# An adaLN block (grouped-KV attention and a ReLU feed-forward): a rewritten start and a rewritten end around an unchanged main loop

## The chip, the cores and the metric

The kernel runs on one core of a Trainium2 chip. A core has five engines that run side by side, each through its own instruction queue in order: TensorE (PE, the matmuls; the loads of its stationary operand are listed apart as PEld), VectorE (DVE), ScalarE (ACT), GpSimd (POOL) and SyncE (SP, which here only starts DMAs). Matmuls write to PSUM, eight banks of 128 x 512 floats; the other engines take the results from there. The metric is the device time of one execution in microseconds (us), the median of several runs. A profile of one execution gives busy times, waits and the TensorE clock that was granted, as a share of full speed.

## What is computed

```python
mod = (silu(c) @ w_mod).reshape(1, 6, 1, 512)       # c: (1, 512), w_mod: (512, 3072)
sa, ca, ga, sb, cb, gb = mod[:, 0] ... mod[:, 5]
h = layernorm(x) * (1 + ca) + sa                    # x: (1, 2048, 512)
# attention: 32 query heads of 16, one head of keys and values for all of them
q, k, v = h @ wq, h @ wk, h @ wv
o = softmax(q @ k.T / 4) @ v
x = x + ga * (o @ wo)
h = layernorm(x) * (1 + cb) + sb
x = x + gb * (relu(h @ w1) @ w2)                    # w1: (512, 1792), w2: (1792, 512)
```

Everything is float32. The kernel keeps that accuracy on the faster matmul type by splitting operands into a high and a low part and adding three products (high x high, high x low, low x high).

## The kernel before

**Tiling.** The 2048 rows are handled in 4 blocks of 512 for the first layer norm and the projections (names `xb1`, `hT`, `kv`, `qproj`), and in 8 blocks of 256 for everything after the attention. A unit `u` is one of 8 query blocks times 4 groups of 8 heads, 32 units in all. A unit needs 64 row maxima (one matmul of 48 x 512 and one DVE reduction over 512 each, `max_of`), then 64 score matmuls with an exponential on ACT (`scores`), and matmuls of the exponentials with the values (`values`).

**Main loop.** 256 cycles `c`, each with 8 maxima for the next unit, 8 scores with their exponentials, 8 matmuls of values, and a portion of "other" work on PE (`behind`: the output projection, second layer norm and feed-forward of the block before). The order within a cycle is written out by hand in `PARTS`: each letter pops one step (a and b a maximum, c and d a score, u and l a portion of other work, V the values, P the steps that were put off, t the transposes). All five engines run exactly in the order of the program text.

**The start (head).** Before the loop: first layer norm, keys and values, the first queries, the six modulation vectors, all 64 maxima of unit 0 and some of unit 1 (`LEAD`, 24). Its order is the string `HEAD`: k is the next step of the generator `first()` (transposes, keys and values, query projections, modulation vectors), n one of `norms()`, m a pair of maxima, w two idle matmuls. The statistics of a row block come from DVE (`ln1_sums`); the inverse root from an integer first guess on DVE and three Newton steps, on POOL (`ln_stats` with `late` false) or on DVE (`late` true). Maxima use three PSUM banks (`ps_max`); the modulation vectors and query projections use the single bank `ps_fill`.

**The end (tail).** `normalise` of the last unit fetches the softmax denominators with small DMAs, all on SP. `behind_last` then does the last block of 256 rows with nothing beside it but the second half of the block before (`second(1)`, 42 matmuls): split of the attention output (`parts`), output projection (24 matmuls), layer norm of one tile of 128 rows after the other, transposes, first layer (14 pieces `f` of 12 matmuls, `dense1`, whose weights `w1s` are fetched by `load_w1` into three buffers), second layer (84 matmuls, `dense2`), `close_block` (residual and store).

**Second modulation.** The scale (1 + cb) and shift sb lie as full tiles `cbr` and `sbr`, made by `mod_all` with a row matmul and a broadcasting matmul each, and `normed` multiplies and adds them row-wise, two operations of 128 x 512 per tile.

The functions that the change touches, and what calls them:

## Time and profile before

| | |
|---|---|
| median of 3 runs | 1687.48 us (1687.15 to 1687.67) |
| the profiled execution, its own time | 1693.38 us |
| its span (first to last record) | 1691.6 us |
| PE busy | 1656.8 us (98% of the span) |
| DVE busy | 1348.8 us (80%) |
| ACT busy | 1229.8 us (73%) |
| POOL busy | 348.0 us (21%) |
| mean granted TensorE clock | 0.982 |
| first score matmul of the loop starts at | 125.35 us |
| last matmul of values ends near | 1607 us |

The span falls into three stages: the head to 125.35 us, the loop to about 1607 us, and the tail to 1691.6 us. A stage table gives for each stretch its length, then for each engine the busy time and the number of instructions, then the granted clock, the busy share of the DMA engines and the rate. A chain row gives a start, a length and the work that the next step waited for. A wait row gives the waiting line, what released it, the total, how often and the longest.

### The profile page before, as it was taken

To read this page: it belongs to the slowest core of one execution; us is meant where nothing else is said; L and a number is where in the kernel's file an instruction comes from. 1 tells how busy PE (TensorE), PEld (TensorE's weight loads), DVE (VectorE), ACT (ScalarE), POOL (GpSimd) and SP (SyncE) were. 2 spreads that over 40 slices of the span, in tenths; PEclk is the share of its full clock that TensorE was granted. 3 is DMA by queue.
4 is the path that set the end of the run, shared out by engine and by line. 5 is a ranking of instruction groups with operands and counts; after the bars stand their busy time and mean duration, and the time that the engine had idled before them with its cause. 6 is when DMAs were issued, how large, how long until landed. Compare 5 with 4: busy or idle time off the path is not lost.

```text
span 1691.6 us, 34294 instructions
## 1 busy us (share of the span) xinstructions
PE 1656.8 (98%) x13196; PEld 967.6 (57%) x13196; DVE 1348.8 (80%) x2327; ACT 1229.8 (73%) x2414; POOL 348.0 (21%) x472
## 2 busy tenths in 40 slices
PE   8899999999999999999999999999999999999987
PEld 6445555555655566556655565556655665556566
DVE  6568888898888888898888888888888888984031
ACT  3318888878877788778877887778877887778710
POOL 3201345431101311121103111131113110221110
PEclk9779999999999999999999999999999999999999
DMA  7122644212301131113311131104211230113132
GB/s 251 54 57 81 198 153 117 89 59 73 105 29 58 34 115 55 35 41 97 91 29 36 59 104 41 59 17 121 66 35 41 85 104 19 45 47 106 30 118 98
DMA packets 86514, 129.13 MB, mean 76 GB/s; under 512 B 24964, under 2 KB 52548, under 8 KB 86352
## 3 DMA queue, kind: packets, MB, share of 16 engines
q1 hardware_dynamic: 84664, 126.85, 24.1%
q8 instruction: 106, 1.74, 0.4%
q14 instruction: 56, 0.46, 0.1%
q10 hardware_dynamic: 1688, 0.08, 0.1%
HBM read 99.94 MB, written 24.76 MB: 74 GB/s over the span
## 4 chain that ended last, share of the span: by engine, by line
PE 92%; DVE 4%; DMA 2%; ACT 1%; POOL 1%; issue 0%; SPq 0%; POOLq 0%; DVEq 0%; ACTq 0%
PE ps_pv L966 29%; PE ps_max L491 22%; PE ps_fill L195 18%; PE ps_exp L785 15%; DVE pm L493 2%; PE ps_max L178 1%; PE ps_exp L178 1%; DMA w1s<-w1dr 1%; PE ps_exp L354 1%; PE ps_fill L178 1%; DVE st L242 1%; PE ps_pv L169 1%; PE ps_exp L329 0%; PE ps_fill L214 0%; ACT pe L787 0%
## 5 line engine op out<-in xcount | busy, mean ns | idle before, releaser
L493 DVE TENSOR_REDUCE pm<-ps_max 128x1 f32<-128x512 f32 x2048 | 1273.1, 683 | 192.2 <-PE ps_fill L195 103.2
L787 ACT ACTIVATE pe<-ps_exp 128x512 f32<-128x512 f32 x2048 | 1081.6, 605 | 297.4 <-PE ps_fill L195 199.9
L491 PE MATMUL ps_max<-kp,qp 48*128 48x512 f32 x2048 | 817.6, 430 | 8.9 <-DVE pm L493 8.7
L785 PE MATMUL ps_exp<-qp,kp 50*128 50x512 f32 x2048 | 746.4, 405 | 0.6 <-ACT pe L787 0.5
L491 PEld LDWEIGHTS ps_max<-kp,qp 48*128 48x128 f32 x2048 | 374.6, 187 | 471.1 <-DVE pm L493 432.6
L966 PE MATMUL ps_pv<-pe,vt 128*32 128x512 f32 x4096 | 546.4, 605 | 0.0
L785 PEld LDWEIGHTS ps_exp<-qp,kp 50*128 50x128 f32 x2048 | 381.9, 187 | 20.8 <-ACT pe L787 5.3
L195 PE MATMUL ps_fill<-w2r,r 64*128 64x512 f32 x1044 | 290.2, 409 | 0.0
L195 PE MATMUL ps_fill<-hh,w1s 64*128 64x256 f32 x1568 | 237.8, 291 | 0.0
L195 PEld LDWEIGHTS ps_fill<-hh,w1s 64*128 64x128 f32 x1568 | 197.3, 185 | 13.4 <-issue 10.1
L195 PEld LDWEIGHTS ps_fill<-w2r,r 64*128 64x128 f32 x1044 | 178.8, 185 | 12.7 <-issue 4.2
L966 PEld LDWEIGHTS ps_pv<-pe,vt 128*32 128x32 f32 x4096 | 80.6, 108 | 126.8 <-issue 119.6
L275 POOL TENSOR_TENSOR r<-stg,r 128x512 fp32r<-128x512 f32 x49 | 63.0, 1285 | 327.8 <-ACT r L274 327.8
L195 PE MATMUL ps_fill<-hl,w1s 64*128 64x256 f32 x784 | 125.3, 280 | 0.0
L195 PE MATMUL ps_fill<-hT,wq 64*128 64x256 f32 x416 | 115.8, 407 | 0.0
L195 PEld LDWEIGHTS ps_fill<-hl,w1s 64*128 64x128 f32 x784 | 107.0, 188 | 0.0
L195 PEld LDWEIGHTS ps_fill<-hT,wq 64*128 64x128 f32 x416 | 70.4, 188 | 2.9
L1011 POOL TENSOR_TENSOR on<-num,den 128x256 f32<-128x256 f32 x31 | 22.8, 735 | 226.5 <-DMA den<-recs 175.1
L801 POOL COPY num<-pvs 128x256 f32<-128x256 f32 x32 | 12.8, 399 | 171.4 <-ACT pvs L797 171.4
L275 POOL TENSOR_TENSOR hl<-stg,hh 128x512 fp32r<-128x512 f32 x14 | 18.0, 1283 | 122.6 <-ACT hh L274 122.6
L282 ACT ACTIVATE stg<-ps_fill 128x512 f32<-128x512 f32 x62 | 38.3, 619 | 0.0
L295 POOL TENSOR_TENSOR x<-stg,x 128x512 f32<-128x512 f32 x14 | 18.1, 1292 | 96.5 <-ACT stg L294 96.5
(163 smaller groups left out, 950.7 us busy)
## 6 DMA issues: line engine op xcount, KB each, us to landing
w1s<-w1dr SPq DMA_DIRECT2D x112, 512.0 KB
qp<-qdr SPq DMA_DIRECT2D x124, 96.0 KB
qdr<-qq SPq DMA_DIRECT2D x45, 256.0 KB
raw<-in_B_w_dram SPq DMA_DIRECT2D x28, 256.0 KB
w1dr<-w1s SPq DMA_DIRECT2D x14, 512.0 KB
wmod<-in_w_mod_dram SPq DMA_DIRECT2D x6, 1024.0 KB
x<-in_A_x_dram SPq DMA_DIRECT2D x8, 512.0 KB
out_dram<-ot SPq DMA_DIRECT2D x16, 256.0 KB
```

The lines of the kernel that those rows point to most:

```text
L169: nc.tensor.matmul(pt[:, 0:P], idn, idn, start=True, stop=True)
L178: nc.tensor.matmul(pt, w, a, start=start, stop=stop)
L195: ins = nc.tensor.matmul(pt, w[r], a[r], start=start and h == 1, stop=stop and h == 0)
L275: (eng or nc.gpsimd).tensor_tensor(lo, src, hi.bitcast(F32), op=OP.subtract)
L282: nc.scalar.activation(stg, pt, func, **kw)
L295: nc.gpsimd.tensor_tensor(dst, stg, other, op=OP.add)
L491: nc.tensor.matmul(pt, qps[u][i][r, j * P:(j + 1) * P], kp[r, kb * 512:(kb + 1) * 512], start=True, stop=True)
L493: nc.vector.tensor_reduce(pms[u][:, (i * 2 + hf) * 4 + j, kb:kb + 1], pt, axis=AX.X, op=OP.max)
L785: nc.tensor.matmul(pt, kp[r, kt * P:(kt + 1) * P], qps[u][ct // 2][r], start=True, stop=True)
L787: nc.scalar.activation(pe, pt, AF.Exp)
L966: nc.tensor.matmul(pvt[i * 32:(i + 1) * 32], vt[:, kt], pes.pop((s, i)), start=(kt == 0), stop=(kt == KT - 1))
L1011: due[1]()
```

## The change

Head: a new string `HEAD` in which nearly every step is followed by a pair of maxima, with further letters: q the first queries, v the last two steps of keys and values, s and a the statistics of blocks 2 and 3, 1, 2 and 3 the normalisation of a tile of that block. The maxima rotate over four banks (`ps_pv` joins in until the loop begins), the steps over four as well (`other_bank`: three `ps_exp` and `ps_fill`). The statistics of block 3 are sums on ACT (`act_sums`: four sums, four sums of squares) instead of DVE. The inverse root is one POOL instruction with the operation pow (`power` holds -0.5) for blocks 1 to 3 and for the second layer norm in the loop; block 0 and the tail keep the Newton steps on DVE. All four normalised tiles of blocks 1 to 3 are POOL's; ACT took some before. The idle matmuls w are gone. `LEAD` is 16, and 8 further maxima of unit 1 run in the first four cycles of the loop, two in each (letter e in `PARTS`).

Second modulation: sb and 1 + cb become columns (`cols`), and `modulate` applies them after the transpose, in the loop with two POOL instructions of 128 x 256 in front of each split (`modulate_two`), in the tail on ACT and DVE.

Tail: the denominators and numerators of the last unit are fetched half by SP and half by the ACT queue, the denominators first, and the last product is on DVE. `behind_last` starts with its loads: the weights of the first 11 pieces `f` go to the three buffers `w1s` and, for 8 pieces, to buffers that held exponentials (`pe`) and queries (`qp`); the other three follow as `w1s` come free. The output projection runs the three ready head groups of both tiles first and the last group after; the layer norm handles both tiles at once; 30 of the 42 matmuls of `second(1)` stand behind the output projection and 12 behind the transposes; the second layer finishes one tile, stores it, and then does the other.

The order of instructions shows it at three places. First PE in the head, where the modulation vectors are made (`L214`/`L216` the row, `L225`/`L234` its broadcast; `L491`/`L516` a maximum; `qp_342` and `qp_451` are unit 0, `qp_739` unit 1; the number behind a bank's name is its use). Before:

```order
L225 MATMUL ps_fill_788<-mrow_780,mean_167 128x512
L491 MATMUL ps_max_791<-kp_109,qp_352 128x512
L491 MATMUL ps_max_794<-kp_109,qp_352 128x512
L214 MATMUL ps_fill_797<-wmod_97,sgb_165 32x512 x4
L491 MATMUL ps_max_804<-kp_109,qp_352 128x512
L491 MATMUL ps_max_807<-kp_109,qp_352 128x512
L225 MATMUL ps_fill_810<-mrow_802,mean_167 128x512
```

and now:

```order
L234 MATMUL ps_fill_793<-mrow_763,mean_167 128x512
L516 MATMUL ps_max_796<-kp_107,qp_451 128x512
L516 MATMUL ps_max_799<-kp_107,qp_451 128x512
L216 MATMUL ps_exp_802<-wmod_495,sgb_165 32x512 x4
L516 MATMUL ps_max_809<-kp_107,qp_451 128x512
L516 MATMUL ps_pv_812<-kp_107,qp_451 128x512
L516 MATMUL ps_max_831<-kp_107,qp_739 128x512
L516 MATMUL ps_max_834<-kp_107,qp_739 128x512
L241 MATMUL ps_exp_837<-idn_101,mrow_785 128x128 x4
```

The broadcast `ps_fill_793` now takes the row of the step before last (`mrow_763`, where `mrow_785` is the newest), other banks alternate with `ps_fill`, every second pair uses `ps_pv`, and the first maxima of unit 1 (`qp_739`) stand between the last row and the two column steps (`L241`) that took the place of two broadcasts.

Second, the DMA starts of SP at the end of the program. Before:

```order
L803 DMA num<-pvs 16x256 x4
L808 DMA den<-pvs 16x256 x4
L605 DMA out_dram<-ot 128x512
L531 DMA x_24355<-in_A_x_dram 128x2x512
L517 DMA w1s<-w1dr_113 128x1024
L517 DMA w1s<-w1dr_114 128x1024
L517 DMA w1s<-w1dr_115 128x1024
L572 DMA out_dram<-ot 128x512
L517 DMA w1s<-w1dr_116 128x1024
```

and now (the loads of `w1x` go on in the same way to `w1dr_121`):

```order
L866 DMA den<-pvs 16x256 x2
L870 DMA num<-pvs 16x256 x2
L558 DMA x_24169<-in_A_x_dram 128x2x512
L544 DMA w1s<-w1dr_111 128x1024
L544 DMA w1s<-w1dr_112 128x1024
L544 DMA w1s<-w1dr_113 128x1024
L700 DMA w1x<-w1dr_114 128x512 x2
L700 DMA w1x<-w1dr_115 128x512 x2
```

The fourth piece of weights stood behind a store that waits for the end of `second(1)`; now 8 more pieces follow the first three directly.

Third, DVE behind the last unit. Before:

```order
L1022 RECIPROCAL den<-den 128x256
L687 TENSOR_TENSOR ol<-on,oh 128x512 x2
L696 TENSOR_TENSOR x_24355<-ps_exp,x_24355 128x512
L242 BN_STATS st<-x_24355 128x6
L243 BN_AGGR mv<-st 128x2
```

and now:

```order
L868 COPY num<-pvs 128x256
L734 TENSOR_TENSOR ol<-on,oh 128x512
L734 TENSOR_TENSOR ol<-on,oh 128x256
L739 RECIPROCAL den<-den 128x256
L739 TENSOR_TENSOR on<-num,den 128x256
L734 TENSOR_TENSOR ol<-on,oh 128x256
L750 TENSOR_TENSOR x_24169<-ps_max,x_24169 128x512 x2
```

The low parts of three head groups no longer stand behind the reciprocal, the product of the last group is DVE's, and both tiles get their residual before the statistics begin.

The diff, cut to its core:

```diff
-LEAD = 24
-HEAD = ("kkmnkkmnnkkmnkmnknnnnk"
-        "kkmnkkmnnkkmkkmkkmkmk" "knnnnmkkm"
-        "kkmkmkmkmkkmkmkmkm"
-        "kmkmkmkmkmkmkmmw"
-        "kmkmkmkmmwmwmwmwmwmwmwmw")
+LEAD = 16
+HEAD = "sq11s1aa1sqmmkkkksakmvm2aq2kq2ak2mmk2kakakam3mk33km3k3mmkvmmkkkmmkkmkmkkmmvkmkmvmkmkmmkmkmkmkmkmkmkmmkmkkmmkmkkmmkkm"
-PARTS = "aucuaucPuaucuadVtbldlbldldlblbcV"
+PARTS = "aucuaucPeuaucuadVtbldlbldldelblbcV"
+NPE = 11
...
+    rot = itertools.cycle([ps_exp, ps_exp, ps_exp, ps_fill])
+    def other_bank():
+        return next(rot)()
...
+    def act_sums(b):
...
+            if t < 4:
+                nc.scalar.activation(scr, xb1[b][:, t], AF.Copy, accum_out=s1[:, t:t + 1])
+            else:
+                nc.scalar.activation(scr, xb1[b][:, t - 4], AF.Square, bias=nm[:, t - 4:t - 3],
+                                     accum_out=s2[:, t - 4:t - 3])
...
-        nc.gpsimd.tensor_scalar(nm, mv[:, :, 0], -1.0, None, op0=OP.mult)
-        for _ in range(3):
-            nc.gpsimd.tensor_tensor(u, y, y, op=OP.mult)
-            nc.gpsimd.tensor_tensor(u, u, ve, op=OP.mult)
-            nc.gpsimd.tensor_scalar(u, u, -0.5, 1.5, op0=OP.mult, op1=OP.add)
-            nc.gpsimd.tensor_tensor(y, y, u, op=OP.mult)
+        if not isinstance(mv, tuple):
+            nc.gpsimd.tensor_scalar(ve, mv[:, :, 1], EPS, None, op0=OP.add)
+            nc.gpsimd.tensor_scalar(nm, mv[:, :, 0], -1.0, None, op0=OP.mult)
+        nc.gpsimd.tensor_tensor(y, ve, power[:, 0:n], op=OP.pow)
...
-        pt = ps_max()
+        pt = next(max_banks)()
...
-            eng.tensor_tensor(xn[:, t], xn[:, t], cbr, op=OP.mult)
-            eng.tensor_tensor(xn[:, t], xn[:, t], sbr, op=OP.add)
+    def modulate(dst, src, k, eng):
+        scale, shift = cols[:, 3, k:k + 1], cols[:, 2, k:k + 1]
...
+    def modulate_two(stg, k2):
+        for k in range(2):
+            v = stg[:, k * TB:(k + 1) * TB]
+            modulate(v, v, k2 * 2 + k, nc.gpsimd)
...
+                    put_off.append(partial(modulate_two, stg, k2))
                     put_off.append(partial(split, flat(parts[0], k2), flat(parts[1], k2), stg))
...
+        ahead += [spare_w1(f, "pe", NPE, nc.sync) for f in range(3, 8)]
+        ahead += [spare_w1(f, "qp", 6, nc.sync) for f in range(8, 11)]
...
+        for t in range(TT):
+            run_all([d for n, d in enumerate(out_proj(pts[t], oo, t)) if n % DC < 3])
+        for t in range(TT):
+            run_all([d for n, d in enumerate(out_proj(pts[t], oo, t)) if n % DC == 3])
+        more(30)
...
-                if f + 3 < FC:
-                    ahead.append(load_w1(f + 3))
+                if f < 3:
+                    ahead.append(load_w1(f + 11))
...
+        if u == NU - 1:
+            nc.gpsimd.tensor_copy(den, pvs[:, TB:])
+            for c in range(4):
+                (nc.sync, nc.scalar)[c % 2].dma_start(
+                    den[c * 32:c * 32 + DH], pvs[c * 32 + DH:(c + 1) * 32, 0:TB])
+            nc.vector.tensor_copy(num, pvs[:, 0:TB])
...
-    sums = [ln1_sums(b) for b in range(NL)]
+    sums = [(ln1_sums, act_sums)[b == 3](b) for b in range(NL)]
...
+    max_banks = itertools.cycle([ps_max, ps_max, ps_max, ps_pv])
...
+        todo_of["e"] = [partial(max_of, *m) for m in extra[:2]]
+        del extra[:2]
...
+    tail = behind_last(NB - 1)
+    next(tail)
     for part in itertools.chain([portion], others, (p for g in carried for p in g)):
...
-    for _, end in ends:
-        end()
-    behind_last(NB - 1)
+    run(tail)
```

## The prediction

> **What bounds the kernel now.** I read the stretches by stage first, then the waits and groups of the head, then the chain of the tail.

> ```profile
> core 0: us, PE busy (x) PEld busy (x) DVE busy (x) ACT busy (x) POOL busy (x), PEclk, DMA share, GB/s
> 16.00:125.35 109.35, 96.45 (x335) 49.92 (x333) 72.40 (x137) 28.05 (x47) 18.93 (x55) 0.80 0.28 94
> 125.35:130.11 4.76, 4.51 (x18) 2.67 (x17) 2.60 (x5) 3.27 (x6) 0.00 (x0) 0.50 0.00 0
> 130.11:133.95 3.84, 3.84 (x24) 1.83 (x23) 1.72 (x4) 1.68 (x4) 0.00 (x0) 0.72 0.02 4
> 135.80:141.50 5.70, 5.70 (x47) 3.29 (x45) 5.00 (x9) 4.16 (x9) 0.00 (x0) 1.00 0.00 0
> 133.95:1607.03 1473.08, 1469.47 (x12375) 843.10 (x12373) 1242.39 (x2096) 1184.63 (x2340) 318.52 (x392) 1.00 0.23 71
> 1607.03:1691.60 84.57, 68.44 (x354) 57.98 (x350) 20.00 (x50) 7.72 (x13) 6.36 (x7) 0.94 0.32 108
> ```

> The loop is PE's: 1469.47 of 1473.08 us at full clock. Nothing in the change takes matmuls out of it, so what can be won lies in the other two stages. The head (to 125.35 us) has PE at a granted clock of 0.80 and DVE busy for 66% only; the tail (84.57 us) has 16.1 us in which PE does nothing, and a clock of 0.94.

> In the head PE and DVE wait for each other:

> ```profile
> DVE pm L493 <- PE ps_max L491: 24.7, 30, 3.8
> ...
> PEld ps_max L491 <- DVE pm L493: 21.7, 27, 2.2
> ```

> ```profile
> L493 DVE TENSOR_REDUCE pm<-ps_max 128x1 f32<-128x512 f32 x88 | 56.1, 684 | 24.7 <-PE ps_max L491 24.7
> L242 DVE BATCH_NORM_STATS2 st<-xb 128x6 f32<-128x512 f32 x12 | 8.1, 678 | 0.0
> L243 DVE BATCH_NORM_AGGREGATE mv<-st 128x2 f32<-128x6 f32 x12 | 2.2, 182 | 0.5
> ...
> L254 DVE TENSOR_SCALAR ve<-mv 128x4 f32<-128x4 f32 x3 | 0.5, 177 | 0.2
> ```

> DVE's 24.7 us of idle time ahead of a maximum is PE coming late with it; PE's weight load waits 21.7 us for a bank that DVE has not emptied. The clock adds to it:

> ```profile
> 28.00:30.00 2.00, 0.35 (x1) 0.18 (x1) 1.97 (x5) 1.15 (x2) 0.00 (x0) 0.97 0.97 378
> 30.00:32.00 2.00, 2.00 (x5) 1.51 (x5) 1.39 (x3) 0.00 (x0) 0.00 (x0) 0.50 0.07 27
> 120.00:130.00 10.00, 9.75 (x35) 6.04 (x35) 6.11 (x10) 3.27 (x6) 0.00 (x0) 0.50 0.11 30
> ```

> After two microseconds in which PE stands still for 1.65, the granted clock falls to 0.50; later it stays there for ten, although PE is busy for 9.75 of them.

> **Head.** DVE's work from 16 us on is 72.4 us. Off it come 8 maxima (8 x 56.1/88 = 5.1), four statistics with aggregates (4 x 0.86 = 3.4) and nine small operations of the first guesses (9 x 0.18 = 1.6); on it go two column reductions and an addition (0.6, priced by the same row). That leaves 62.9 us, so DVE can't end the head before 16 + 62.9 = 78.9. PE's 96.45 us at 0.80 are 77 us at full clock, an upper figure: the 36 idle matmuls and 8 maxima are still in it, and busy ends are modelled.

> How dense will it be? Below, DVE keeps its present 66%: 16 + 62.9/0.66 = 111.3 us. Above, 100%: 78.9. I take the share that DVE has in a full cycle of the loop, 5.00 of 5.70 us = 0.877, because the new order has what that cycle has: a maximum between nearly all steps and enough banks (four instead of three; a pair needs two, so with four the next pair starts while DVE empties the first). 16 + 62.9/0.877 = **87.7 us**, 37.6 less than 125.35.

> Two waits in it are new. The load of unit 1's queries now stands close to its use: seven pairs and six steps lie between the last of that projection and the first maximum of unit 1, 14 maxima on DVE at 0.64 or some 9 to 10 us with the rest. Today the way through DRAM takes

> ```profile
> 52.19 1.97 SPq L388 DMA_DIRECT2D qdr<-qq  x3
> 59.38 1.77 SPq L438 DMA_DIRECT2D qp<-qdr  x4
> ```

> from 52.19 to 61.15 until the last read is issued (the one at 59.38 waited for the write to land), and the split lies ahead of it. So PE may stop for 1 to 2 us there, the length after which the clock fell above; one spell of up to ten microseconds at half clock costs up to 5 us, which the distance between 78.9 and 87.7 holds. And the roots by pow: no row has this operation. Below stands a POOL operation on two inputs of 128x2:

> ```profile
> 552.06 0.19 POOL L266 TENSOR_TENSOR u<-y 128x2 f32<-128x2 f32 x1 [0.39 <-DVE y L256]
> ...
> 561.10 1.28 POOL L550 TENSOR_TENSOR xn<-xn,sbr 128x512 f32<-128x512 f32 x1
> 572.49 0.38 ACT L590 ACTIVATE stg<-ps_max 128x256 f32<-128x256 f32 x1
> 576.57 0.63 ACT L274 ACTIVATE hh<-stg 128x512 fp32r<-128x512 f32 x1
> ```

> 0.19 us, and above 1.28 us, that of 512 elements. I take 0.5, by the first row, for 4 elements are near 2; it replaces twelve of them, so each block of the head gains about 2 us on POOL, which the two tiles that POOL takes over from ACT use up. The sums on ACT are hidden: ACT is busy 28 of 109 us there.

> [...] The rows show 0.50 after a stop of 1.65 us. [...]

> **First cycles.** DVE has 10 maxima instead of 8 in four cycles: 5.00 x 10/8 = 6.25 us against 5.70, so 0.55 x 4 = 2.2 us more. Against that, the loop's first 8.60 us ran at 0.50 and 0.72; two halves of a full cycle take 5.70, so 2.9 us come back if PE arrives at full clock. Together -0.7 us (between -2.9 and +2.2).

> **Loop.** Two POOL products per split are new, ahead of ACT's `hh`, and ACT, PE and DVE would queue behind it. Above, the stage tile is written at 572.87 and ACT takes it at 576.57: 3.7 us cover for two operations of 128x256, under 1.28 us together. If that cover went, the excess would fall on exponentials, 14 times. Seven roots by pow have the 10 us between the end of `xn` (562.4) and the transposes (ahead of 572.49) as cover, and four row products less per block (4 x 1.28). I cost both at nothing.

> **Tail.** What ends last today:

> ```profile
> 1612.77 1.84 DMA den<-pvs
> ...
> 1618.32 2.58 PE ps_exp L178 x10
> ...
> 1624.97 0.56 DVE xn L547
> ...
> 1647.74 4.35 DMA w1s<-w1dr
> ...
> 1653.87 6.21 DMA w1s<-w1dr
> ...
> 1667.68 19.38 PE ps_max L178 x83
> ```

> The fetch of the denominators, the layer norm and twice the weights stand in it. One piece of the first layer starts 1.51 us after the one before:

> ```profile
> 1646.04 1.19 PE L178 MATMUL ps_exp<-hh,w1s 128*128 128x256 f32 x8 [1.14 <-DMA w1s<-w1dr]
> ...
> 1647.55 1.19 PE L178 MATMUL ps_exp<-hh,w1s 128*128 128x256 f32 x8
> ```

> PE's own work: 174 matmuls of 512 columns (24 + 42 + 24 + 84) at 19.38/83 = 0.2335 are 40.6 us; 14 pieces at 1.51 are 21.1; eight transposes about 1. Sum 62.7, against 80.0 from 1607.03 to 1687.06, the end of the last 83.

> Which waits remain? The last head group: 4 fetches on each of two queues, denominators first, so the last of these starts near 1609.0 instead of 1612.77 and lands 1.84 later; reciprocal, product, high and low part take what they take now on this chain (1614.61 to 1618.32, 3.7) and end by 1615. PE needs them only after 24 + 18 matmuls, at 1616.8. ACT now starts four of the fetches ahead of its splits: half of the eight that SP had started by 1612.77, so it is through near 1610.6, before the 24 matmuls end at 1612.6. The layer norm: one tile takes 4.1 us from its matmuls (1620.90) to `xn` (1624.97); for both together only residual and statistics come twice, under half of that. From the end of the output projection at 1618.2 that is 6 us and a tile's 0.56, done near 1625; the 30 matmuls placed there last to 1625.2. The 12 others (2.8 us) cover the split. Weights: 0.5 + 5.6 MB from about 1611 at the rate of this tail,

> ```profile
> 1650.00:1660.00 10.00, 5.84 (x45) 5.23 (x43) 1.96 (x3) 1.19 (x2) 0.00 (x0) 1.00 0.85 271
> ```

> 271 GB/s, are there by 1634; the first layer begins at about 1629 and reaches its eleventh piece at 1644. So PE ends near 1607.03 + 62.7 + 0.5 = 1670.2. Behind it lie 4.5 us today, with two residuals and two stores; I take 3.8 with one of each. The tail takes 67.0 instead of 84.57: **-17.6 us**, between -11.4 (one wait of 6.21 for weights remains) and -18.

> **Sum.** -37.6 - 0.7 - 17.6 = -55.9 on a span of 1691.6, so 1635.7. The profiled execution's own time is 1693.38, the median 1687.48; the difference lies outside the stages, so I take it off the median: 1631.6, or **1632 us**.

> **Rivals.**
> *DVE's share doesn't rise* (0.14): the banks were not what held it, and PE's half clock goes on to the loop. Head 111.3, first cycles +2.2: -14.1 + 2.2 - 17.6 = -29.5, 1658. For it: PE and DVE have nearly equal sums, so each stop hits both. Against: most of DVE's idle time is before maxima.
> *PE never falls to half clock* (0.14): head near 81, -44.4 - 0.7 - 17.6 = -62.7, 1625. [...]
> *A stop at the first pow* (0.07): block 1's tiles wait for it as long as for the twelve operations it replaces (at 0.19 and a gap, some 3.3 us), PE has nothing else in its queue, and 8 us of half clock follow, +4: +7, 1639. For it: the operation is new to POOL. Against: no row here shows a first use that pays. [...]
> *The weights still end last in the tail* (0.06): the two waits of the chain, 4.35 and 6.21, come back in the new place, tail -7: 1642. For it: SP starts the new loads one behind the other, each waiting for a buffer of the loop. Against: those buffers are read last by 1607.
> *Slower: pow is a slow routine* (0.03). Place: POOL, three times ahead of the tiles in the head, seven times ahead of `xn` in the loop. Price p each: 3p in the head, in the loop 7 times what exceeds its cover of about 17 us (10 and the products that fall away). Faster turns to slower where 3p + 7(p - 17) = 55.9, at p = 17.5 us, thirteen times the 1.28 of 512 elements. At 20 us: 1714.
> *It doesn't do what it says* (0.02): the order moves but the stages end as before, 1687.

> **Numbers.** The forecast has 0.54; its own range, 1626 to 1642. For 8 in 10 the range reaches up to the first rival: 1621 to 1657. 0.2% (3.4 us) is about what a measurement can tell from no change: faster 0.95, same 0.02, slower 0.03.

> **What would show it.** The first score matmul at 84 to 94 us with a clock over 0.9 between 45 us and there; DVE idle ahead of maxima well under 24.7; the pow row under 1.3 us; cycles 0 to 3 near 6.3 us; no wait of `hh` on POOL; no wait of PE on w1 in the tail, and 67 us from the last values to the end. Wrong would be: a head above 105, half clock after 45 us for over 15 us, or a loop that differs from 1473 us by over 5.

## The result, and the profile after

The changed kernel takes **1634.18 us** (median of 4 runs, 1632.62 to 1635.61) against 1687.32 us (1686.76 to 1687.67) for the kernel before on the same chip: a ratio of 0.9685, 95% interval 0.9668 to 0.9702. The prediction was 1632 us. The profiled execution has a span of 1632.5 us (its own time 1634.79) against 1691.6.

The stage times below compare these two profiled executions. That of the kernel before is a long one: its 1693.38 us lie 5.9 above the median, so the stages differ by 59.1 us where the medians differ by 53.1.

The stretches by stage, changed kernel (columns as in the prediction; the rows end at the first score matmul, the second and the ninth group of value matmuls, the last value matmul, and PE's last matmul):

```profile
16.00:86.10 70.10, 66.78 (x298) 36.21 (x298) 59.48 (x113) 27.06 (x56) 20.11 (x31) 0.98 0.36 122
86.10:93.35 7.25, 6.53 (x43) 3.38 (x40) 6.65 (x11) 5.63 (x11) 0.00 (x0) 1.00 0.52 121
93.35:116.10 22.75, 22.68 (x159) 10.88 (x157) 21.12 (x36) 16.57 (x33) 3.86 (x3) 1.00 0.24 68
116.10:1565.60 1449.50, 1449.25 (x12226) 833.20 (x12225) 1221.25 (x2047) 1168.27 (x2308) 284.26 (x319) 1.00 0.23 72
1565.60:1627.39 61.79, 61.41 (x350) 53.36 (x350) 19.27 (x43) 8.90 (x16) 2.83 (x3) 1.00 0.39 143
1627.39:1632.50 5.11, 0.00 (x0) 0.00 (x0) 0.69 (x1) 0.00 (x0) 0.00 (x0) 0.99 0.14 53
```

The same cuts through the loop of the kernel before:

```profile
125.35:133.95 8.60, 8.35 (x41) 4.50 (x40) 4.33 (x8) 4.95 (x10) 0.00 (x0) 0.60 0.01 2
133.95:153.91 19.96, 19.96 (x152) 11.38 (x150) 17.39 (x29) 16.36 (x34) 3.82 (x3) 1.00 0.12 32
153.91:1607.03 1453.12, 1449.51 (x12225) 831.72 (x12223) 1225.00 (x2068) 1168.28 (x2308) 314.70 (x390) 1.00 0.24 72
```

| stage | before, us | after, us | difference | predicted |
|---|---|---|---|---|
| to the first score matmul | 125.35 | 86.1 | -39.3 | -37.6 |
| from there to the second group of values | 8.60 | 7.25 | -1.35 | -2.9 |
| to the ninth | 19.96 | 22.75 | +2.8 | +2.2 |
| the rest of the loop | 1453.12 | 1449.50 | -3.6 | 0 |
| last values to the end | 84.57 | 66.9 | -17.7 | -17.6 |
| sum | 1691.6 | 1632.5 | -59.1 | -55.9 |

PE is now busy for 95% of the head (66.78 of 70.10 us) at a granted clock of 0.98. Its waits with DVE, in the list of waits from 16 to 86.1 us (total, times, longest), have shrunk, DVE's most:

```profile
PEld ps_max L516 <- DVE pm L518: 12.7, 19, 1.9
...
DVE pm L518 <- PE ps_max L516: 2.4, 4, 1.7
DVE pm L518 <- PE ps_pv L516: 1.9, 3, 0.8
PE ps_max L516 <- DMA qp<-qdr: 1.6, 1, 1.6
```

DVE waits 2.4 + 1.9 us for maxima instead of 24.7. The last row is the one long stop of PE in this head: it ends at 74.28 us, when the queries of unit 1 are back from DRAM. Behind it the clock falls once (windows of 3.41 us, cut where the clock changes):

```profile
72.53:75.94 3.41, 1.82 (x11) 1.04 (x10) 2.93 (x7) 0.69 (x2) 0.25 (x1) 1.00 0.38 117
75.94:79.35 3.41, 3.41 (x12) 2.22 (x12) 1.69 (x7) 0.00 (x0) 0.00 (x0) 0.50 0.04 5
```

The chain of the tail has no transfer in it any more (start, duration, work):

```profile
1565.55 5.71 PE ps_fill L175 x24
1571.26 5.61 PE ps_max L175 x24
1576.87 7.00 PE ps_fill L175 x30
1583.87 0.45 PE ps_exp L172 x4
...
1588.23 19.90 PE ps_exp L175 x165
1608.13 19.26 PE ps_max L175 x84
...
1627.41 0.69 DVE ot L608
```

### The profile page after: what moved, and what is told of

Same layout as the page of the kernel before. It is cut to its first block, busy times and chain, and to the rows that moved or that the text cites. A ratio compares the mean times of both kernels' runs of the same rounds, so it can differ in the third digit from the quotient of the medians.

```text
span 1632.5 us, 34097 instructions
## 1 busy us (share of the span) xinstructions
PE 1619.8 (99%) x13164; PEld 948.1 (58%) x13164; DVE 1337.9 (82%) x2287; ACT 1230.6 (75%) x2425; POOL 315.2 (19%) x374
## 3 DMA queue, kind: packets, MB, share of 16 engines
q8 instruction: 105, 1.72, 0.4%
## 4 chain that ended last, share of the span: by engine, by line
PE 94%; DMA 2%; DVE 1%; ACT 1%; POOL 1%; SPq 0%; issue 0%; ACTq 0%; POOLq 0%
PE ps_pv L1024 31%; PE ps_max L516 22%; PE ps_fill L192 21%; PE ps_exp L846 15%; PE ps_max L175 2%; PE ps_exp L175 1%; PE ps_fill L175 1%; DVE pm L518 1%; DMA xb<-in_A_x_dram 1%; DMA qdr<-qq 0%; PE ps_max L188 0%; ACT pe L848 0%; DMA wkv<-in_A_wk_dram 0%; SPq L97 0%; DMA recs<-rc 0%; PE ps_exp L378 0%
## 5 line engine op out<-in xcount | busy, mean ns | idle before, releaser
L518 DVE TENSOR_REDUCE pm<-ps_max 128x1 f32<-128x512 f32 x2028 | 1259.8, 683 | 168.4 <-PE ps_fill L192 110.6
L516 PE MATMUL ps_max<-kp,qp 48*128 48x512 f32 x2028 | 809.4, 424 | 1.9 <-DMA qp<-qdr 1.6
L516 PEld LDWEIGHTS ps_max<-kp,qp 48*128 48x128 f32 x2028 | 371.9, 186 | 456.2 <-DVE pm L518 424.6
L1024 PEld LDWEIGHTS ps_pv<-pe,vt 128*32 128x32 f32 x4096 | 80.5, 108 | 125.4 <-issue 118.1
L299 POOL TENSOR_TENSOR r<-stg,r 128x512 fp32r<-128x512 f32 x49 | 62.9, 1283 | 328.5 <-ACT r L298 321.5
L192 PE MATMUL ps_fill<-wol,oh 64*128 64x512 f32 x112 | 38.0, 418 | 0.0
```

The lines of the kernel that those rows point to most:

```text
L192: ins = nc.tensor.matmul(pt, w[r], a[r], start=start and h == 1, stop=stop and h == 0)
L299: (eng or nc.gpsimd).tensor_tensor(lo, src, hi.bitcast(F32), op=OP.subtract)
L516: nc.tensor.matmul(pt, qps[u][i][r, j * P:(j + 1) * P], kp[r, kb * 512:(kb + 1) * 512], start=True, stop=True)
L518: nc.vector.tensor_reduce(pms[u][:, (i * 2 + hf) * 4 + j, kb:kb + 1], pt, axis=AX.X, op=OP.max)
L1024: nc.tensor.matmul(pvt[i * 32:(i + 1) * 32], vt[:, kt], pes.pop((s, i)), start=(kt == 0), stop=(kt == KT - 1))
```

## The experiments

All are edits of the changed kernel, except one of the kernel before. Stage times are from one profiled execution each, and all of them vary by themselves. The four kernels below that leave the head as it is (guess_loop, no_spare, old_fetch, old_norm) reach the first score matmul at 85.8 to 87.4 us: the two with one spell of 3.41 us at half clock at 85.8 and 86.0, the two with 6.83 us at 87.1 and 87.4. Kernels with the same loop and no half clock in it show 1477.0 to 1479.5 us for it. The span ends 3.7 to 5.1 us behind PE's last matmul. So the tail is compared up to that matmul: 80.0 us before, 61.8 in the changed kernel, and 61.8 to 62.2 in the eight experiments that leave its end as it is.

| kernel | first score matmul, us | half clock in the head, us | last values to PE's last matmul, us | span, us |
|---|---|---|---|---|
| before | 125.4 | 44 | 80.0 | 1691.6 |
| changed | 86.1 | 3.4 | 61.8 | 1632.5 |
| fill_before | 124.6 | 25 | 76.8 | 1688.4 |
| grouped | 109.0 | 20.5 | 61.8 | 1656.4 |
| banks3 | 99.3 | 10.2 | 61.8 | 1643.6 |
| early_q | 91.5 | 10.2 | 61.8 | 1637.6 |
| lead24 | 89.1 | 6.8, on into the loop | 61.8 | 1633.1 |
| sums_dve | 85.6 | 0 | 62.2 | 1628.7 |
| half_q | 83.5 | 0 | 61.8 | 1628.3 |
| banks5 | 83.1 | 0, then 6.8 in the loop | 61.8 | 1629.5 |

### What shortened the head: the clock, the order or the banks?

**The kernel before, with its stops filled (fill_before).** At the places of the long stops (behind the first maxima, ahead of the transposes of blocks 2 and 3 in `tr1_now`, ahead of the values' transposes in `kv`, between the last maxima):

```diff
     ln1(1, 1, nc.gpsimd)
+    warm(7, ps_pv)
     pairs(1)
...
+            if b > 1 and k == 0:
+                warm(6, ps_pv)
...
+        if b:
+            warm(6, ps_pv)
...
-        "kmkmkmkmmwmwmwmwmwmwmwmw")
+        "kmkmkmkmmwwmwwmwwmwwmwwmwwmwwmww")
```

> The kernel before, with idle matmuls of 128x128 put into the places where PE stood still for over a microsecond ahead of a spell of half clock (seven behind the first maxima, six in the keys of each block and ahead of the transposes of blocks 2 and 3, four instead of two between the last maxima). Theory A (half clock is the cause: 43.9 of the 109 us from 16 to 125.35 were at half clock): with the stops filled the clock stays up and the first score matmul comes at 103 to 113 us instead of 125.35. Theory B (the order and the waits between PE and DVE are the cause, the clock follows from them): not before 120 us. An idle matmul that holds PE while a bank is free costs up to 4 us in all.

Measured: first score matmul at 124.6 us. The windows of this kernel show that the clock did come back for most of the head:

```profile
31.50:34.90 3.40, 3.40 (x14) 2.51 (x13) 0.90 (x3) 0.47 (x1) 0.00 (x0) 0.50 0.00 0
34.90:103.00 68.10, 62.79 (x301) 33.76 (x299) 50.65 (x93) 21.71 (x34) 11.43 (x35) 1.00 0.15 44
103.00:124.60 21.60, 21.19 (x70) 14.69 (x70) 9.01 (x14) 0.00 (x0) 0.00 (x0) 0.50 0.28 80
```

25 us at half clock instead of 44, and 0.8 us gained. That is what theory B forecast, but it does not price the clock, for the 0.8 us is net of what the fillers themselves cost. Idle matmuls keep PE busy for 28.9 us between 16 and 124.6 us, where the kernel before has 9.6; how much of that held up other work was put at 4 us and not measured.

The kernel before itself suggests that half clock was worth more. It ran 25 times beside these experiments. Its span falls from 1690.9 us at a mean granted clock of 0.982 to 1679.9 at 0.990, and over all 25 it follows the clock closely: about 0.34 us for each us at half clock, an estimate by a straight line through them. At a clock of 0.989, that of fill_before, the kernel before has spans of 1681.4 and 1682.5 us and fill_before 1688.4. Where in the program those executions lost their clock is not recorded. If the head's 44 us were worth the same, some 14 of its 39 us are the clock's. So it is not shown how the head's gain divides between the clock and the waits that bring it down.

**Grouped maxima (grouped).** Same steps, same maxima, same banks, another string:

```diff
-HEAD = "sq11s1aa1sqmmkkkksakmvm2aq2kq2ak2mmk2kakakam3mk33km3k3mmkvmmkkkmmkk..."
+HEAD = "sq11s1aa1sqkkkksakvmmmm2aq2kq2ak2k2kakaka3mmmmk33k3k3kvmmmmkkkkkmmmm..."
```

> The changed kernel with the same steps and maxima in the head, but the 40 pairs of maxima put together in ten groups of four pairs between the steps. Theory (the order makes the head dense): a group is 8 x 0.68 = 5.4 us of DVE, four banks hold half of it, so PE waits about 2.7 us in each group and DVE idles in the steps between: 13 us more, and spells of half clock of 3.41 us each on top; first score matmul at 96 to 110 us. Rival (what counts is the work taken off DVE, and the banks): within 3 us of 86.1.

Measured: 109.0 us, +22.9, with 20.5 us at half clock. From its list of waits (16 to 109 us, DVE):

```profile
DVE pm L518 <- PE ps_max L516: 8.8, 7, 2.7
DVE qp L451 <- ACT ql L450: 7.9, 3, 3.3
DVE qq L418 <- ACT qq L417: 6.1, 2, 5.2
DVE vt L397 <- PE ps_exp L395: 6.0, 2, 4.3
```

DVE now idles between the groups, also ahead of small operations behind a step. The theory holds, inside the 96 to 110 us that it gave: the order, with the clock that it keeps up, is worth more than half of the head's gain. The 17.1 us more at half clock can account for up to 8.5 of the 22.9 (half of them: in the kernel before, eight matmuls of values took 1.93 us at a clock of 0.50, at 130.12 us, and 1.06 at 1.00, at 1606.04); by that count at least 14 are the order's by itself.

**Three banks (banks3).**

```diff
-    max_banks = itertools.cycle([ps_max, ps_max, ps_max, ps_pv])
+    max_banks = itertools.cycle([ps_max])
```

> The changed kernel with three banks for maxima in the head instead of four. Theory (banks are part of what lets DVE run densely): PE's weight loads wait longer than their 13.7 us for a bank and the first score matmul comes 3 to 8 us later, at 89 to 94 us. Rival (the order alone, one pair of maxima between nearly all steps, does it): within 1 us of 86.1.

Measured: 99.3 us, +13.2, well above the expected 3 to 8. Its waits (16 to 100 us):

```profile
PE ps_max L516 <- DVE pm L518: 9.0, 12, 3.4
...
PEld ps_max L516 <- DVE pm L518: 24.3, 32, 3.8
```

The weight loads wait 24.3 instead of 12.7 us, and PE itself stops for 9.0, so two spells of half clock come on top, 6.8 us more than in the changed kernel and up to 3.4 of the 13.2. The fourth bank is needed for the order to work; the two effects are not to be added (grouped and banks3 undo partly the same thing).

**Five banks (banks5)**, on top of half_q (below):

```diff
+    rot = itertools.cycle([ps_exp])
...
-    max_banks = itertools.cycle([ps_max, ps_max, ps_max, ps_pv])
+    max_banks = itertools.cycle([ps_max, ps_max, ps_max, ps_pv, ps_fill])
```

> The kernel half_q (unit 1's queries in two halves) with five banks for maxima in the head instead of four: the bank of the loop's fill steps joins them, and the other steps of the head keep three. Taking one bank away cost 13.2 us. Theory (PE's remaining waits for a bank, 11.0 us on the weight loads of half_q, are still lost time): one bank more brings 2 to 5 us, first score matmul at 79 to 81.5 instead of 83.5 us. Rival (with four banks PE is busy through nearly all of the head and is the bound now): within 1 us of 83.5, or later by up to 2 where the other steps miss the bank.

Measured: 83.1 us, -0.4; 1632.22 us (1631.35 to 1633.44, 5 runs), ratio 0.9688 (0.9664 to 0.9712). The rival: the weight loads' waits for a bank fell only from 11.0 to 4.8 + 3.0 + 1.8 us, and PE waited 1.2 and 1.1 us for a result of DVE and of ACT instead. A spell of half clock at the loop's start took back what was left. The fifth bank was taken from the other steps, and those two waits are theirs; what a bank on top of all would bring is not shown.

**Block 3's sums on DVE (sums_dve).**

```diff
-    sums = [(ln1_sums, act_sums)[b == 3](b) for b in range(NL)]
+    sums = [ln1_sums(b) for b in range(NL)]
```

> The changed kernel, with block 3's sums on DVE (four statistics and aggregates, 4 x 0.86 = 3.4 us) instead of ScalarE. Theory of the prediction (the head is DVE's work at a share, 0.85 in the changed kernel): 3.4/0.85 = 4.0 us more, first score matmul at 90.1 us. Rival (DVE has slack where these sums stand, or PE sets the pace there): under 1.5 us more.

(`HEAD` loses four of its eight letters "a".) Measured: 85.6 us. It had no spell of half clock, although PE stops at the same maximum:

```profile
PE ps_max L516 <- DVE negm L522: 1.6, 1, 1.6
```

A spell of 3.41 us costs up to 1.7 us, and by the kernels with one and two of them 1.0 to 1.6. So 3.4 us of work given back to DVE cost some 0.5 to 1.5 us and not 4.0. The rival holds: DVE's sum does not set the head.

**16 or 24 maxima ahead (lead24).**

```diff
-LEAD = 16
+LEAD = 24
...
-    extra = [(*places[0][:1], hf, *places[0][1:], kb) for kb in range(KB) for hf in (1, 0)]
-    places = places[1:]
+    extra = []
```

> The changed kernel with 24 maxima of unit 1 ahead, as before the change, and none added to the first four cycles: the head ends with four pairs more. Theory of the prediction (a maximum in the head costs DVE's time at its share): 8 x 0.68/0.85 = 6.4 us more in the head, first score matmul at 92.5 us; the first four cycles come back to 5.70 us from 6.5, 3.2 less; net +3.2 us. Rival (the cheaper one is PE's time, 0.49 for a pair): 2.0 us more in the head, net -1.2.

(`HEAD` ends with four pairs more.) Measured: first score matmul at 89.1 us, +3.0; the first eight groups of values after the first take 23.0 instead of 26.0 us. That would be a draw; the span is 0.6 us longer, which single executions can't tell from none. Neither price was right: 3.0 us in the head lie between the 6.4 of DVE at its share and the 2.0 of PE. With nothing between the last pairs PE stops again, and the clock falls across the loop's start as it did before (windows of this kernel):

```profile
84.00:86.00 2.00, 0.77 (x4) 0.40 (x4) 1.56 (x4) 0.60 (x1) 0.00 (x0) 1.00 0.05 11
86.00:88.00 2.00, 1.78 (x4) 0.85 (x4) 2.00 (x4) 0.00 (x0) 0.00 (x0) 0.81 0.47 112
```

### The one stop that is left

**Unit 1's queries first (early_q).** `first()` projects them ahead of block 3's transposes; in `HEAD` the last step of block 3's keys moves ahead of one pair.

```diff
         for b in range(1, NL):
+            if b == 3:
+                yield from qproj_now(0, 1, other_bank, True)
+                load_q(1)
             yield from tr1_now(b)
...
-            if b == 3:
-                yield from qproj_now(0, 1, other_bank, True)
-                load_q(1)
```

> The changed kernel, with the queries of unit 1 projected ahead of block 3's transposes instead of behind its keys, eight steps earlier. Theory (PE is what the stop costs): the 1.59 us stop of PE at 72.69 us, where it waits for the read of those queries, goes, and with it the one spell of half clock (3.41 us, worth 1.7): first score matmul at 82.8 instead of 86.1 us, no half clock in the head, time 1631 us (-3.3). Rival (DVE sets the head's pace and works on through the stop): only DVE's idle 1.68 us at 79.3 comes back, first score matmul not before 84.4, time within 1.7 us of 1634.

Measured: both theories missed. First score matmul at 91.5 us, 1639.58 us (1635.5 to 1642.63, 4 runs; ratio 0.9713, 0.9677 to 0.9749). The stop at 72.69 is gone, and a longer one stands at block 3's keys, whose last step lost the steps that had covered it:

```profile
PE ps_max L516 <- POOL kp L389: 2.6, 1, 2.6
...
PEld ps_max L516 <- POOL kp L389: 3.4, 1, 3.4
```

with three windows of 3.41 us at half clock behind it. The four steps of that projection were the cover of the keys; I had looked only at what waits for the queries.

**The half that is needed first (half_q).** The order stays, the projection is cut:

```diff
-                yield from qproj_now(0, 1, other_bank, True)
+                yield from qproj_now(0, 1, other_bank, True, None, 0, TB)
                 load_q(1)
+                yield from qproj_now(0, 1, other_bank, True, None, TB)
```

(`qproj` gets an upper bound `n1` beside `n0`, for its matmuls, the split and the three writes.)

> The changed kernel, with the projection of unit 1's queries cut in two: the half that unit 1 uses (256 of 512 columns) is written to DRAM and read back right behind its own two steps, two steps and four pairs of maxima earlier than now; the order of steps and maxima stays. Theory (the stop of 1.59 us and its one spell of half clock are lost time): the stop goes and no spell of half clock is left in the head; first score matmul at 82.8 us, time -3.3 us (1631). Rival (the head's length follows from the order of steps and maxima, other waits take the place of this one): the stop goes, but the first score matmul stays within 1 us of 86.1.

Measured: 83.5 us, no half clock (a mean clock of 1.000 in all five runs), **1629.38 us** (1628.85 to 1630.71, 5 runs; before on the same chip 1687.12), ratio 0.9656 (0.9634 to 0.9678). 2.6 of the 3.3 us came.

```profile
16.00:83.50 67.50, 66.40 (x299) 35.63 (x298) 59.45 (x114) 27.28 (x57) 20.18 (x31) 1.00 0.37 126
```

PE is busy for 66.40 of 67.50 us here: it is the head's bound now. This is the fastest version of the study. It wasn't timed beside the changed kernel on one chip; their runs do not overlap, the intervals of their ratios just do.

### The loop's 3.6 us

In the kernel before, PE's waits from 153.91 us to the last values are 3.2 us in seven stops (list of waits), once per block:

```profile
PE ps_max L491 <- DVE pm L493: 3.2, 7, 0.5
```

One of them in the timeline of that kernel: three small operations of the first guess stand between the maxima on DVE, and PE waits for the bank behind them:

```profile
551.40 0.17 DVE L254 TENSOR_SCALAR ve<-mv 128x2 f32<-128x2 f32 x1
...
551.60 0.17 DVE L255 TENSOR_SCALAR y<-ve 128x2 int32<-128x2 int32 x1
551.81 0.17 DVE L256 TENSOR_SCALAR y<-y 128x2 int32<-128x2 int32 x1
...
552.62 0.50 PE L491 MATMUL ps_max<-kp,qp 48*128 48x512 f32 x1 [0.47 <-DVE pm L493]
```

**Guesses back on DVE in the loop (guess_loop).**

```diff
+        if n == TT:
...
+            nc.vector.tensor_scalar(ve, mv[:, :, 1], EPS, None, op0=OP.add)
+            nc.vector.tensor_scalar(yi, ve.bitcast(I32), 1, None, op0=OP.logical_shift_right)
+            nc.vector.tensor_scalar(yi, yi, -1.0, float(0x5f3759df), op0=OP.mult, op1=OP.add)
...
+            return nm, y
         if not isinstance(mv, tuple):
```

> The changed kernel, with the seven roots of the loop as before the change: the first guess in three operations of 0.17 us on DVE, the rest on POOL. In the kernel before, PE stood still seven times for 0.46 us in the loop, each time ahead of a maximum behind these three operations; in the changed kernel it doesn't. Theory (these small DVE operations cost PE that time): seven stops of about 0.46 us are back, and the stretch from the first score matmul to the end of the last values is 1482.7 instead of 1479.5 us. Rival (the stops came from elsewhere, the modulation on DVE's or ACT's way, say): no such stops, 1479.5 within 0.5.

(The three Newton steps stay on POOL.) Measured: 1483.0 us instead of 1479.5 (1477.0 to 1479.5 in all kernels without them), and the stops are back, in number and length:

```profile
PE ps_max L529 <- DVE pm L531: 3.2, 7, 0.5
```

(The added lines shift the numbers by 13.) So pow's gain in the loop is not POOL's time but 0.5 us of DVE's, seven times.

### The tail

**Without the spare weight buffers (no_spare):**

```diff
-        ahead += [spare_w1(f, "pe", NPE, nc.sync) for f in range(3, 8)]
-        ahead += [spare_w1(f, "qp", 6, nc.sync) for f in range(8, 11)]
...
-                if f < 3:
-                    ahead.append(load_w1(f + 11))
+                if f + 3 < FC:
+                    ahead.append(load_w1(f + 3))
```

> The changed kernel without the eight loads of first-layer weights into buffers that have become free (three buffers in turn, as before). Theory (the two waits of the chain of before, 4.35 and 6.21 us, are taken away by the spare buffers and by nothing else): they come back, with up to one spell of half clock; the stretch from the last values to the end is 77 to 79 instead of 66.9 us. Rival (the weights waited for work that has become earlier, the buffers matter little): under 3 us more.

Measured: 73.9 us to the end, 68.8 to PE's last matmul: +7.0, between the two. In its waits from the last values on, and below them in those of the kernel before (1607.03 to 1690 us):

```profile
PE ps_exp L175 <- DMA w1s<-w1dr: 4.8, 6, 1.5
...
PE ps_exp L178 <- DMA w1s<-w1dr: 5.7, 5, 3.0
```

PE waits for weights again, in more and shorter stops than before and without half clock. The theory had read the chain's 4.35 and 6.21 us as stops of PE; they are how long the transfers ran. PE stood still for 5.7 us in the kernel before, in five stops, so 10.6 could not come back. Of the 7.0 us, 4.8 are stops; the rest is a busy time of PE that is 2.1 us longer (63.5 against 61.4 us).

**The old fetch (old_fetch)**: SP's queue alone, numerators first, product on POOL.

```diff
-            for c in range(4):
-                (nc.sync, nc.scalar)[c % 2].dma_start(
-                    den[c * 32:c * 32 + DH], pvs[c * 32 + DH:(c + 1) * 32, 0:TB])
...
+            for c in range(4):
+                nc.sync.dma_start(num[c * 32 + DH:(c + 1) * 32], pvs[c * 32:c * 32 + DH, TB:])
+            nc.gpsimd.tensor_copy(den, pvs[:, TB:])
+            for c in range(4):
+                nc.sync.dma_start(den[c * 32:c * 32 + DH], pvs[c * 32 + DH:(c + 1) * 32, 0:TB])
```

> The changed kernel with the fetch of the last unit's numerators and denominators as before: eight transfers on SP's queue, denominators last, the product on GpSimd. In the changed kernel the last low part is ready at 1574.51 and PE takes it at 1575.2, 0.6 us of slack. Theory (the two queues and the order are needed for that): the denominators land 2.4 to 3 us later, the product takes 0.6 longer, PE stops 2 to 3 us ahead of the last piece of the output projection, and the stretch from the last values to the end is 69 to 71.5 instead of 66.9 us. Rival (other slack takes it up): under 0.7 us more.

Measured: 67.9 us to the end, 63.5 to PE's last matmul, +1.7, between the two (+1.0 to the end, where 4.4 us lie behind PE instead of 5.1). Two stops where the theory put them, shorter than it said:

```profile
PE ps_max L175 <- ACT oh L730: 0.8, 1, 0.8
...
PE ps_max L175 <- DVE ol L734: 0.3, 1, 0.3
```

**One tile after the other (old_norm):**

```diff
-        more(30)
-        mv = ln_mv(TT)
...
+        more(12)
+        for t in range(TT):
+            pt = ps_exp()
+            run_all(out_proj(pt, oo, t))
+            V.tensor_tensor(x1[:, t], pt, x1[:, t], op=OP.add)
+            mv = ln_mv(1)
+            ln_sums(mv, 0, x1[:, t])
+            normed(x1, xn, [t], *ln_stats(mv, 1, True), V if t == 0 else nc.gpsimd)
+        more(99)
```

> The changed kernel with the layer norm of the last block one tile after the other, each behind its own output projection, and twelve matmuls of the block before ahead of them instead of thirty behind. Theory (the norm is hidden behind matmuls either way): the stretch from the last values to the end stays within 1.5 us of 66.9. Rival (taking both tiles through the norm together is itself a part of the tail's gain): PE stops ahead of the transposes as it did before (3.9 us there), 3 to 6 us more.

Measured: 69.4 us, 65.5 to PE's last matmul: +3.7, the rival (+2.5 to the end, where 3.9 us lie behind PE instead of 5.1). The stop stands one step later than it said, at the first layer behind the split (waits from the last values on):

```profile
PE ps_exp L175 <- ACT hh L580: 2.3, 3, 1.2
```

The three add up to 7.0 + 1.7 + 3.7 = 12.4 of the 18.2 us between 80.0 and 61.8; they were undone singly, not together. The rest was not taken apart. The tail before has two spells of half clock, 6.8 and 3.4 us long, which would account for up to 5.1 of it. Part of that shows in fill_before, whose tail has the same program and only one spell of 3.4: 76.8 us, 3.2 less, with PE busy for 66.0 instead of 68.4 us and waiting 1.1 us less for weights.

## Why the prediction was right, and where it was not

**Head (-37.6, measured -39.3).** The number is right, its reason only in part, and so the number is partly luck. Order and banks make the head dense, as said: undoing either costs 22.9 and 13.2 us, the half clock that comes with it included. The removed idle matmuls, the roots by pow and the tiles on POOL were not undone singly in the head. But the step "DVE's work at the loop's share" fails: DVE's work was 59.48 us instead of 62.9, its share 0.85 instead of 0.877, the two errors work against each other, and sums_dve shows that work added to DVE does not come out at its price. DVE does not even end this head: its last pair of maxima and one `qq`, 2.0 us, lie behind the first score matmul. What sets the end is PE. Its 96.45 us at a clock of 0.80, called an upper figure of 77 at full clock, were 66.4 us when nothing stopped it; the prediction had the row and set no term from it.

**New waits.** The stop at unit 1's queries was forecast at 1 to 2 us and is 1.59; the spell at half clock was forecast at up to ten and is 3.41 in the profiled execution. The four timed executions have mean clocks of 0.997 to 1.000 and spans of 1630.5 us (at 1.000, without a spell) to 1633.2. Half clock after 45 us was to stay under 15 us; it came to 3.41. The 81 us that the rival without half clock gives to the head no run shows; heads without half clock ended at 83.1 (banks5), 83.5 (half_q) and 85.6 us (sums_dve).

**pow (taken as 0.5, bounds 0.19 and 1.28).** The groups by shape of the changed kernel:

```profile
L293 POOL TENSOR_TENSOR y<-ve,power 128x2 f32<-128x2 f32 x7 | 5.1, 730 | 0.0
L293 POOL TENSOR_TENSOR y<-ve,power 128x4 f32<-128x4 f32 x2 | 2.1, 1044 | 0.0
L293 POOL TENSOR_TENSOR y<-ves,power 128x4 f32<-128x4 f32 x1 | 1.0, 1036 | 0.1
```

0.73 us for two columns and 1.04 for four, the first use included: no stop at the first pow, so that rival is out, and so is the slow routine (p = 17.5 us; for p = 20 its sum gives 1713, not 1714).

**First cycles (-0.7, measured +1.4).** The starts of the value matmuls (every second group is a cycle):

```profile
90.05 1.07 PE L1024 MATMUL ps_pv<-pe,vt 128*32 128x512 f32 x8
...
96.66 1.07 PE L1024 MATMUL ps_pv<-pe,vt 128*32 128x512 f32 x8
...
116.10 1.06 PE L1024 MATMUL ps_pv<-pe,vt 128*32 128x512 f32 x8
...
121.80 1.06 PE L1024 MATMUL ps_pv<-pe,vt 128*32 128x512 f32 x8
```

A cycle with ten maxima takes 6.6 us (26.05/4 = 6.5 over the four, with the passage to 5.70), not 6.25. The term counted DVE's two maxima; PE is busy for 22.68 of 22.75 us there, so the two cost PE's time, some 0.45 us each. The other half was over-sized too: at the loop's start 1.3 us came back, not 2.9, because PE stops for some 0.7 us in the first stretch (6.53 of 7.25) and that stretch has extra maxima too.

**Loop (0, measured -3.6).** Inside the 5 us allowed, but not nothing: the step that costed the roots at nothing looked at POOL's cover and not at the three DVE operations that they replaced (guess_loop). The modulation on POOL costs nothing, as said: 28 operations of 0.555 us, and no wait of `hh` for POOL in the loop.

**Tail (-17.6, measured -17.7).** PE's only stop in the list of waits is 0.4 us, for `hh`. There is no wait for weights and none for the last head group, whose slack (the high part ready at 1574.06, loaded by PE at 1575.08) is 1.0 us where the prediction had 1.8. PE's own work came to 61.8 instead of 63.2 us, because pieces of the first layer follow each other in 1.42 us (19.90/14), not 1.51; and 5.1 us lie behind PE's last matmul, not 3.8 (3.7 to 5.1 in all kernels here). These two offset each other. The bound of -11.4 and the rival of the weights took 6.21 and 10.6 us as PE's waits, where PE waited 5.7 in all. The three undone parts show that each edit costed there had a share.

**From span to median.** The span came out 3.2 us shorter than predicted, the median 2.2 us longer. The step between them fails. The 5.9 us taken off do not lie outside the stages: the profiled execution's own time is only 1.8 us above its span. They are those of one long execution, with a mean clock of 0.982 where the 25 others have 0.981 to 0.991, and so part of the stages' 59.1 us; the changed kernel's profiled execution is only 0.6 us above its median. Without this step the forecast would have been 1637.5 us, 3.3 too long instead of 2.2 too short. That the two errors met is luck.

## What to carry to other kernels

When two engines feed each other through a few buffers, spread the small producer-consumer pairs between all other steps and give them one buffer more than a pair's turn needs, before counting either engine's work; the first extra bank was worth 13 us here with its clock, the next, taken from the other steps, nothing. A step that is moved takes its cover with it: look at what it had been hiding where it stood (early_q) as well as at what waits for it. And operations of 0.2 us on an engine that is 84% busy (1225.00 of 1453.12 us in the loop before) are not free when the bound engine waits for its next result: three of them cost 0.46 us each time.

## What the runs showed of the hardware

```profile
71.06:74.47 3.41, 2.69 (x14) 0.55 (x13) 3.09 (x6) 1.29 (x3) 0.00 (x0) 1.00 0.28 89
74.47:77.88 3.41, 2.53 (x15) 1.85 (x16) 3.06 (x9) 0.23 (x1) 0.25 (x1) 1.00 0.25 70
```

In guess_loop and no_spare, whose heads are those of the changed kernel, the stop left PE 1.64 and 1.66 us idle inside one window (busy for 1.77 and 1.75 of 3.41), and half clock followed each time. So in these heads a stop of about half a window was enough. The prediction read a stop of 1.65 us as a length that trips. By these runs it is a matter of where the stop falls, too: half clock followed 1.59 us inside one window and did not follow 1.60 us across two.

**Busy time alone does not decide.** The share of busy time in a window does not foretell the next one's clock: banks5 has a window with PE busy for 1.81 us and no spell behind it, where the changed kernel's 1.82 us had one. In grouped the window ahead of a spell has 2.66, and a PE that is busy throughout can stay at half (6.70 of 6.80 us). The first row is of banks5, the others of grouped:

```profile
24.24:27.65 3.41, 1.81 (x15) 1.34 (x14) 1.57 (x5) 3.07 (x8) 0.61 (x1) 1.00 1.04 384
...
28.39:31.80 3.41, 2.66 (x12) 1.17 (x11) 2.60 (x5) 2.07 (x6) 2.55 (x6) 1.00 0.96 353
31.80:38.60 6.80, 6.70 (x14) 4.36 (x14) 2.92 (x6) 0.47 (x1) 2.00 (x3) 0.50 0.02 7
```

In fill_before PE is busy for 21.19 of 21.60 us with maxima and idle matmuls and stays at 0.50 for all of it. Whether it is the kind of matmul that counts (maxima use 48 of 128 rows), or that busy ends are modelled, stays open.
